# Attention and feed-forward kernel on one core: a shorter prologue, copies moved to ScalarE, and a new rule for filler matmuls

## Chip, cores and metric

One core of a Trainium2 (trn2) chip. The metric is device time in microseconds (us) of one execution, taken over several executions. A run counts as slow when it is over 1.5% above the fastest run of the same kernel; only fast runs are compared here unless a sentence says otherwise. A span (first to last instruction of the profiled execution) is about 2 us shorter than the device time of the same run (1036.2 against 1037.95 us before, 1008.3 against 1010.06 after).

Engine names as the profile prints them: PE is TensorE (matmuls), PEld its weight loads, ACT is ScalarE, DVE is VectorE, POOL is GpSimd, SP is the engine that issues most DMAs (27 of the 29 on the page of the kernel before).

## The reference, cut to what matters

```python
# x: [1, 2048, 512] bf16; 32 query heads of 16, one shared K/V head of 16; F = 1792
xn = layernorm(x)
q = (xn @ wq) -> 32 heads;  k = xn @ wk;  v = xn @ wv
p = softmax(q k^T * 16**-0.5)          # 32 x 2048 x 2048 exponentials
s = (p v) @ wo
g = silu(silu(xn @ w1) @ w2)
out = x + s * g
```

The softmax needs 32 x 2048 x 2048 exponentials, and ScalarE computes all of them.

## The kernel before

The sequence is cut into 4 chunks of 512 queries; four heads make a group, so there are 8 groups per chunk. A **unit** is a piece of the scores: 4 PSUM banks (even units) or 2 banks (odd units), 512 columns per bank. There are 683 units. Even units use banks 0 to 3, odd units banks 4 and 5; bank 6 gathers the output of a group, bank 7 serves **jobs**: all other matmul work (Q of later chunks `q`, both feed-forward layers `h` and `z`, output projection `w`), cut into parts of two matmuls that are strewn between units.

In each step PE computes the scores of unit idx+2, multiplies the finished exponentials of unit idx by V, and does a job part if one is due:

```python
for idx in range(min(2, NU)):
    emit_S(idx, NFILL_START)             # 3 fillers
for idx in range(MAXU):
    if idx < NU:
        if idx + 2 < NU:
            emit_S(idx + 2, nfill_for(idx))
        emit_PV(idx)
    for (n, pi) in parts_at_unit.get(idx, []):
        emit_job_part(n, pi)

def emit_S(u, nfill=0):
    if u >= 2:
        pe.wait_ge(act_sem.sem, u - 1)   # exp of unit u-2 has emptied these banks
    # ... 4 or 2 score matmuls; then, into the last bank:
    for fi in range(nfill):              # a zero weight: adds 0, costs PE time
        h = pe.matmul(bank(b0 + k), lhsT=zero_sb, rhs=xnT_sb[:, 0, 0:NQ], start=False, ...)
    h.then_inc(s_sem.sem, 1)             # the exp of unit u waits for this

def nfill_for(idx):
    nmm = sum(len(job_parts[n][pi]) for (n, pi) in parts_at_unit.get(idx, []))
    target = NFILL_START if idx < N_START else (NFILL if idx <= last_part_unit else NFILL_TAIL)
    return max(0, target - nmm)          # 3 at the start, 1 in the middle, 2 in the tail
```

A **filler** is a matmul with a zero weight. It keeps PE busy (0.39 us is recorded for one, 0.82 for three in a row, in the timelines below), and it stands between the scores and the semaphore that lets their exp begin. (The fillers of scores u are chosen from the job parts at step u-2.)

ScalarE's loop is one exp per unit, and a tanh (for the feed-forward part) behind some of them:

```python
a.wait_ge(s_sem.sem, u + 1)
a.activation(p_sb[...], ps[:, b0 * 512:(b0 + n) * 512], ACT.Exp).then_inc(act_sem.sem, 1)
for jn in cons_at_unit.get(u, []): emit_tanh(jn)
```

The prologue before these loops: layer norm, transposes of half 0 of the tokens, K of half 0, V, Q of group 0; then the same for half 1, with K and V in banks 0 to 2 again; then Q of groups 1 to 5 through banks 3 and 4. VectorE does every copy out of PSUM. Groups 6 and 7 of Q are jobs.

```python
NGP = 6 if NT > NT0 else NG
NGB = min(NGP, 3)
# ... PE:
for g in range(NGB, NGP):
    pe.wait_ge(qev_sem.sem, g)           # VectorE has copied the last Q out of bank 3
    emit_Q(g, 3)
qev_needed_for_bank = {2 + g: g + 1 for g in range(1, NGB)}
if NGP > NGB:
    qev_needed_for_bank[3] = NGP         # unit 0 needs bank 3
```

The softmax here doesn't subtract the row's maximum and nothing guards it: scores larger than these inputs give would overflow.

## Time and profile before

The first timing gave 1038.83 us (median of 5 runs, 1035.72 to 1043.29). The profiled execution has a span of 1036.2 us:

| stretch of the profiled execution | us |
|---|---|
| start to exp 0 | 47.51 |
| exp 0 to the start of the last exp | 974.01 |
| last exp to the end | 14.64 |

From the page of the kernel before. The first lines give busy time and its share of the span. The two rows of digits show the busy tenths of ACT and the granted PE clock in 40 slices of the span. The lower lines are groups of instructions: line, engine, operation, output and input, shape, count, then busy us and mean ns, then idle time of the engine just before them.

```profile
span 1036.2 us, 12801 instructions
...
PE 812.2 (78%) x5323; PEld 223.8 (22%) x5426; DVE 201.3 (19%) x356; ACT 972.6 (94%) x776; POOL 10.4 (1%) x13
...
ACT  4199999999999999999999999999999999999994
...
PEclk9999999999999999999989999999978999999999
...
L522 ACT ACTIVATE p_sb<-ps 128x1024 bf16<-128x1024 f32 (+1 forms) x683 | 949.8, 1573 | 36.4 <-PE ps L628 26.6
...
L628 PE MATMUL ps<-xnT_sb,zero_sb 128*128 128x512 bf16 x435 | 153.7, 392 | 2.7 <-issue 2.7
```

ACT is busy 94% of the time, and of its 36.4 us of idle time before exps 22.3 came before the first. The 78% of PE is not a sign of a full PE: 153.7 us of it are the fillers of L628.

**ScalarE's floor.** The records of single exps overlap: a four-bank exp's lasts 1998 ns on average, but the next exp can start 1757 ns after it. What counts is the distance from one start to the next, read from the trace's start times: 1757 ns after a four-bank exp, 904 ns after a two-bank exp, 477 ns after a tanh, when nothing is late. The trace has 341 four-bank and 342 two-bank exps, and the last, a two-bank one, has no distance after it: 341 x 1757 + 341 x 904 + 72 x 477 ns = 941.7 us. What a distance has above these values is called **excess** below. Summed over the stage the excess is 32.1 us: 0.9 in units 0 to 5, 17.3 in units 6 to 572, 13.8 in units 573 to 682, where no jobs are left.

The end of the prologue, timeline of the kernel before. Columns: start us, duration us, engine, line, operation, output and input, shape, count, and in brackets how long the engine was idle before and what released it.

```profile
34.33 2.56 PE L550 MATMUL ps<-xnT_sb,wkp_sb 128*128 128x512 bf16 x8 [2.58 <-DVE xnT_sb L361]
...
37.97 2.11 PE L566 MATMUL ps<-xnT_sb,wqp_sb 128*128 128x512 bf16 x7 [0.23 <-issue]
...
44.51 1.04 PE L566 MATMUL ps<-xnT_sb,wqp_sb 128*128 128x512 bf16 x4 [0.78 <-DVE qT_sb L375]
...
45.58 0.69 DVE L375 TENSOR_SCALAR qT_sb<-ps 128x512 bf16<-128x512 f32 x1 [1.13 <-PE ps L566]
...
46.33 0.39 PE L622 MATMUL ps<-qT_sb,kT_sb 32*128 32x512 bf16 x1 [0.46 <-DVE qT_sb L375]
...
47.51 2.79 ACT L522 ACTIVATE p_sb<-ps 128x2048 bf16<-128x2048 f32 x2 [22.28 <-PE ps L628]
```

K of half 1 begins at 34.33 us. Q group after Q group follows, each waiting for VectorE to copy out the one before (the bracket of the line at 44.51 names `DVE qT_sb`). Three of unit 0's four score matmuls start; the fourth, at 46.33, waits for the last Q to leave bank 3. The exp follows at 47.51.

One pair of units in the tail, timeline of the kernel before. The two lines of L622 with x4 are the starts of two consecutive four-bank scores:

```profile
1006.05 0.39 PE L622 MATMUL ps<-qT_sb,kT_sb 32*128 32x512 bf16 x4 [0.46 <-ACT p_sb L522]
...
1006.37 0.61 PE L628 MATMUL ps<-xnT_sb,zero_sb 128*128 128x512 bf16 x2
...
1008.95 0.40 PE L622 MATMUL ps<-qT_sb,kT_sb 32*128 32x512 bf16 x4 [0.46 <-ACT p_sb L522]
```

A pair takes 2.90 us here, against 1757 + 904 ns = 2.66 us of ScalarE work. In the start times of the exps the distance after a two-bank exp is 1128 ns in this stretch, 224 late. In units 495 to 504, which have no jobs either but one filler instead of two, it is 913.

Stretches of the kernel before. Columns: stretch and its length, busy us and instructions of PE, PEld, DVE, ACT and POOL, then the mean granted PE clock, the DMA share and GB/s:

```profile
746.00:766.00 20.00, 14.19 (x102) 4.18 (x102) 3.41 (x6) 20.00 (x17) 0.00 (x0) 1.00 0.00 0
766.00:786.00 20.00, 19.53 (x85) 3.83 (x86) 2.79 (x5) 17.64 (x13) 0.00 (x0) 0.50 0.00 1
884.00:1012.00 128.00, 105.56 (x691) 27.29 (x702) 11.17 (x20) 122.62 (x89) 0.00 (x0) 1.00 0.00 1
```

From 766 to 786 us the granted clock is a half. In those 20 us ACT is busy only 17.64. The clock records hold five such spells inside the exp stage, 37.5 us together; the longest, 20.5 us, is this one.

### The profile page before, as it was taken

The page shows a single profiled execution, that of the slowest core. Times are in us where ns is not written, and L with a number is a line of the kernel's source. Part 1 is how long each engine was busy: PE and PEld are TensorE (multiplying, and loading weights), DVE is VectorE, ACT ScalarE, POOL GpSimd, SP SyncE. Part 2 cuts the span into 40 slices and gives each one's busy share as a digit, 9 for nine tenths or more (in the row PEclk, how much of TensorE's full clock was granted, in tenths as well). Part 3 has the DMA queues.
Part 4 walks back from the last instruction along what each step waited for, and adds up shares of the span by engine and source line. Part 5 has one row for each costly group of instructions (what it writes and reads, how often), then busy time and mean ns, then how long its engine had stood idle before and what let it go on. Part 6 is the DMA issues. An engine that isn't in the chain of part 4 may idle for free.

```text
span 1036.2 us, 12801 instructions
## 1 busy us (share of the span) xinstructions
PE 812.2 (78%) x5323; PEld 223.8 (22%) x5426; DVE 201.3 (19%) x356; ACT 972.6 (94%) x776; POOL 10.4 (1%) x13
## 2 busy tenths in 40 slices
PE   1787778777788887778888877778889888888886
PEld 1322222222222222222222222222222222222222
DVE  7312222211211222121112212221101211100112
ACT  4199999999999999999999999999999999999994
POOL 4000000000000000000000000000000000000000
PEclk9999999999999999999989999999978999999999
DMA  9000000000000000000000000000000000000000
GB/s 265 1 1 1 1 1 1 1 1 1 1 1 6 16 2 1 1 1 1 1 1 16 6 1 1 1 1 2 1 1 11 11 1 1 1 1 1 2 1 20
DMA packets 7369, 9.76 MB, mean 9 GB/s; under 512 B 1488, under 2 KB 6608, under 8 KB 7312
## 3 DMA queue, kind: packets, MB, share of 16 engines
q1 hardware_dynamic: 6576, 5.28, 1.9%
q0 software_dynamic: 736, 3.67, 1.0%
q8 instruction: 42, 0.69, 0.3%
q14 instruction: 15, 0.12, 0.0%
HBM read 6.85 MB, written 2.10 MB: 9 GB/s over the span
## 4 chain that ended last, share of the span: by engine, by line
ACT 46%; PE 35%; issue 14%; DVE 4%; DMA 0%; ACTq 0%; another core or an unknown queue 0%; DVEq 0%
ACT p_sb L522 43%; PE ps L622 12%; PE ps L647 9%; PE ps L628 6%; ACT t_sb L512 3%; PE ps L686 2%; PE ps L679 2%; PE ps L711 1%; PE ps L692 1%; DVE stats_sb L337 1%; DVE oraw_sb L396 1%; PE ps L550 1%; PE ps L739 1%; PE ps L566 1%; DVE xnT_sb L361 0%
## 5 line engine op out<-in xcount | busy, mean ns | idle before, releaser
L522 ACT ACTIVATE p_sb<-ps 128x1024 bf16<-128x1024 f32 (+1 forms) x683 | 949.8, 1573 | 36.4 <-PE ps L628 26.6
L622 PE MATMUL ps<-qT_sb,kT_sb 32*128 32x512 bf16 x2048 | 272.3, 391 | 167.1 <-ACT p_sb L522 163.8
L647 PE MATMUL ps<-p_sb,vaug_sb 128*32 128x512 bf16 x2048 | 278.7, 396 | 16.4 <-DVE oraw_sb L396 7.9
L628 PE MATMUL ps<-xnT_sb,zero_sb 128*128 128x512 bf16 x435 | 153.7, 392 | 2.7 <-issue 2.7
L622 PEld LDWEIGHTS ps<-qT_sb,kT_sb 32*128 32x128 bf16 x2048 | 66.7, 91 | 412.5 <-ACT p_sb L522 383.7
L647 PEld LDWEIGHTS ps<-p_sb,vaug_sb 128*32 128x32 bf16 x2048 | 68.8, 93 | 193.0 <-issue 151.7
L431 DVE SCALAR_TENSOR_TENSOR u_sb<-t_sb,ps 128x512 bf16<-128x512 bf16 x56 | 38.3, 684 | 246.3 <-ACT t_sb L512 246.3
L396 DVE CAST oraw_sb<-ps 128x512 bf16<-128x512 f32 x32 | 22.1, 691 | 252.4 <-PE ps L647 252.4
L686 PE MATMUL ps<-w_sb,u_sb 128*128 128x512 bf16 x208 | 64.8, 387 | 3.8 <-issue 2.1
L679 PE MATMUL ps<-xnT_sb,w_sb 128*128 128x512 bf16 x203 | 64.1, 389 | 0.2 <-issue 0.2
L512 ACT ACTIVATE t_sb<-ps 128x512 bf16<-128x512 f32 x72 | 58.6, 815 | 0.0
L628 PEld LDWEIGHTS ps<-xnT_sb,zero_sb 128*128 128x128 bf16 x482 | 37.1, 96 | 85.5 <-issue 84.8
L442 DVE TENSOR_SCALAR qT_sb<-ps 128x512 bf16<-128x512 f32 x26 | 17.9, 688 | 107.7 <-PE ps L692 87.9
L435 DVE SCALAR_TENSOR_TENSOR tmp_sb<-t_sb,ps 128x512 bf16<-128x512 bf16 x16 | 10.9, 680 | 141.0 <-ACT t_sb L512 141.0
L692 PE MATMUL ps<-xnT_sb,wqp_sb 128*128 128x512 bf16 x93 | 29.9, 394 | 0.5 <-issue 0.5
L711 PE MATMUL ps<-wop_sb,xn_sb 128*128 128x512 bf16 x91 | 29.2, 400 | 0.8 <-issue 0.8
L415 DVE SCALAR_TENSOR_TENSOR fin_sb<-ps,tmp_sb 128x512 bf16<-128x512 f32 x16 | 11.0, 687 | 61.7 <-PE ps L711 58.3
L398 DVE STREAM_TRANSPOSE otr_sb<-oraw_sb 128x512 bf16<-128x512 bf16 x32 | 22.8, 712 | 1.1
L411 DVE STREAM_TRANSPOSE xn_sb<-otr_sb 128x512 bf16<-128x512 bf16 x32 | 22.8, 711 | 1.1
L686 PEld LDWEIGHTS ps<-w_sb,u_sb 128*128 128x128 bf16 x224 | 12.7, 97 | 27.8 <-issue 25.4
L679 PEld LDWEIGHTS ps<-xnT_sb,w_sb 128*128 128x128 bf16 x224 | 12.8, 97 | 25.7 <-issue 25.7
L539 PE MATMUL ps<-ident,xn_sb 128*128 128x128 bf16 x64 | 5.5, 266 | 12.7 <-DVE xn_sb L353 12.7
(46 smaller groups left out, 128.2 us busy)
## 6 DMA issues: line engine op xcount, KB each, us to landing
w_sb<-in_B_w_dram POOLq DMA_DIRECT2D x2, 1792.0 KB, 14.0
x_sb<-in_A_x_dram SPq DMA_DIRECT2D x4, 512.0 KB, 5.4
out_dram<-ob_sb SPq DMA_DIRECT2D x16, 128.0 KB, 1.7
wqn_sb<-in_A_wq_dram SPq DMA_DIRECT2D x1, 512.0 KB, 7.8
wop_sb<-in_A_wo_dram SPq DMA_DIRECT2D x4, 128.0 KB, 7.5
wkn_sb<-in_A_wk_dram SPq DMA_DIRECT2D x1, 16.0 KB, 6.8
wv_sb<-in_A_wv_dram SPq DMA_DIRECT2D x1, 16.0 KB, 6.5
```

The source lines that it names most:

```text
L396: v.tensor_copy(oraw_sb[:, sl, :], bank(OB)).then_inc(o_sem.sem, 1)
L398: v.transpose(otr_sb[:, sl, :], oraw_sb[:, sl, :]).then_inc(dv.sem, 1)
L431: v.scalar_tensor_tensor(out=u_sb[:, tc % 2, ft, :], in0=t_sb[:, ti % 2, :], scalar=1.0, in1=bank(FB), op0=ALU.add, op1=ALU.mult).then_inc ...
L512: a.activation(t_sb[:, ti % 2, :], bank(FB), ACT.Tanh, scale=scale).then_inc(t_sem.sem, 1)
L522: a.activation(p_sb[:, u % NPB, 0:n * NQ], ps[:, b0 * 512:(b0 + n) * 512], ACT.Exp).then_inc(act_sem.sem, 1)
L622: h = pe.matmul(bank(b0 + k), lhsT=kT_sb[32 * i:32 * i + KP, kt * P:(kt + 1) * P], rhs=qT_sb[32 * i:32 * i + KP, c % 2, g, :], start=True, ...
L628: h = pe.matmul(bank(b0 + k), lhsT=zero_sb[:, :], rhs=xnT_sb[:, 0, 0:NQ], start=False, stop=(fi == nfill - 1))
L647: h = pe.matmul(bank(OB)[32 * i:32 * (i + 1), :], lhsT=vaug_sb[:, kt, :], rhs=p_sb[:, u % NPB, k * NQ:(k + 1) * NQ], start=(kt == 0), stop ...
L679: h = pe.matmul(bank(FB), lhsT=w1_sb[:, dc, ft * P:(ft + 1) * P], rhs=xnT_sb[:, dc, tc * NQ:(tc + 1) * NQ], start=(dc == 0), stop=(dc == N ...
L686: h = pe.matmul(bank(FB), lhsT=u_sb[:, tc % 2, ft, (tt % 4) * P:(tt % 4 + 1) * P], rhs=w2_sb[:, ft, :], start=(ft == 0), stop=(ft == NFT - 1))
L692: h = pe.matmul(bank(FB), lhsT=wqp_sb[:, dc, g, :], rhs=xnT_sb[:, dc, c * NQ:(c + 1) * NQ], start=(dc == 0), stop=(dc == NDC - 1))
L711: h = pe.matmul(bank(FB), lhsT=on_sb[:, (c % 2) * NG + g, (tt % 4) * P:(tt % 4 + 1) * P], rhs=wop_sb[:, g, :], start=(g == 0), stop=(g == ...
```

## The change

Three things at once. (1) Only Q of groups 0 and 1 is computed ahead of the loop; groups 2 to 5 become jobs. (2) Half 1 uses banks of its own (4 to 7), and ScalarE, not VectorE, copies V, Q and the K of half 1 out of PSUM; waits for these copies are placed where a bank or value is first used. (3) A unit step without job parts gets 1 filler if even and 3 if odd.

```diff
-    NGP = 6 if NT > NT0 else NG
-    NGB = min(NGP, 3)
+    BIG = NT > NT0
+    NGP = 2 if BIG else NG
@@ VectorE: the copies of V, Q and half-1 K are removed @@
@@ ScalarE, after its normalisation work and the load of the Exp table @@
+            a_evac_V(0, 2)
+            a_evac_Q(0, 3)
+            if BIG:
+                for c in range(NC0, NC):
+                    a.wait_ge(kp_sem.sem, c + 1)
+                    a.activation(kT_sb[:, c * NQ:(c + 1) * NQ], bank(4 + c - NC0), ACT.Copy).then_inc(kev2_sem.sem, 1)
+                a_evac_V(1, 6)
+                a_evac_Q(1, 7)
@@ PE @@
                 for c in range(NC0, NC):
-                    emit_K(c, c - NC0)
-                emit_V(1, 2)
-                for g in range(1, NGB):
-                    emit_Q(g, 2 + g)
+                    emit_K(c, 4 + c - NC0)
+                emit_V(1, 6)
+                emit_Q(1, 7)
-            for g in range(NGB, NGP):
-                pe.wait_ge(qev_sem.sem, g)
-                emit_Q(g, 3)
@@ waits for banks 4 to 7 and for half 1 of K and V move to their first use (cut) @@
             def nfill_for(idx):
                 nmm = sum(len(job_parts[n][pi]) for (n, pi) in parts_at_unit.get(idx, []))
+                if nmm == 0:
+                    return 1 if idx % 2 == 0 else 3
                 target = ...
             for idx in range(min(2, NU)):
-                emit_S(idx, NFILL_START)
+                emit_S(idx, 1 if idx == 0 else NFILL_START)
```

More of the change, by code (lines that the diff above doesn't have):

```diff
@@ L266, in bass_recurrent_scan__grouped_kv_mqa__dense_activation_silu__prompt_kernel @@
         kev_sem = S_("kev")
+        kev2_sem = S_("kev2")
         vp_sem = S_("vp")
@@ L361, in evac_T @@
                     v.tensor_copy(xnT_sb[:, dc, ta * P:tb * P], src_).then_inc(xt_sem.sem, 1)
-            def evac_K(c, b):
-                v.wait_ge(kp_sem.sem, c + 1)
-                v.tensor_copy(kT_sb[:, c * NQ:(c + 1) * NQ], bank(b)).then_inc(kev_sem.sem, 1)
-            def evac_V(half, b):
-                ta, tb = halves[half]
-                v.wait_ge(vp_sem.sem, half + 1)
-                vps = bank(b).rearrange("p (t e) -> p t e", e=32)[:, 0:tb - ta, 0:DH]
-                v.tensor_copy(vaug_sb[:, ta:tb, 0:DH], vps).then_inc(vev_sem.sem, 1)
-            def evac_Q(g, b):
-                v.wait_ge(qp_sem.sem, g + 1)
-                v.tensor_scalar(qT_sb[:, 0, g, :], bank(b), QSCALE, None, op0=ALU.mult).then_inc(qev_sem.sem, 1)
             evac_T(0)
             for c in range(NC0):
-                evac_K(c, c)
-            evac_V(0, 2)
-            evac_Q(0, 3)
+                v.wait_ge(kp_sem.sem, c + 1)
+                v.tensor_copy(kT_sb[:, c * NQ:(c + 1) * NQ], bank(c)).then_inc(kev_sem.sem, 1)
             if len(halves) > 1:
                 evac_T(1)
-                for c in range(NC0, NC):
-                    evac_K(c, c - NC0)
-                evac_V(1, 2)
-            for g in range(1, NGB):
-                evac_Q(g, 2 + g)
-            for g in range(NGB, NGP):
-                evac_Q(g, 3)
             marks["xt_total"] = NDC * len(halves)
@@ L500, in _, with a_evac_V, a_evac_Q @@
             a.activation(scr_sb[:, 0:1], rstd_sb[:, 0:1], ACT.Exp)
+            def a_evac_V(half, b):
+                ta, tb = halves[half]
+                a.wait_ge(vp_sem.sem, half + 1)
+                vps = bank(b).rearrange("p (t e) -> p t e", e=32)[:, 0:tb - ta, 0:DH]
+                a.activation(vaug_sb[:, ta:tb, 0:DH], vps, ACT.Copy).then_inc(vev_sem.sem, 1)
+            def a_evac_Q(g, b):
+                a.wait_ge(qp_sem.sem, g + 1)
+                a.activation(qT_sb[:, 0, g, :], bank(b), ACT.Copy, scale=QSCALE).then_inc(qev_sem.sem, 1)
+            a_evac_V(0, 2)
[6 more added lines that the diff above has]
+                a_evac_Q(1, 7)
+            else:
+                for g in range(1, NGP):
+                    a_evac_Q(g, 3)
             def emit_tanh(n):
@@ L574, in _ @@
             emit_Q(0, 3)
-            if len(halves) > 1:
+            if BIG:
                 emit_transposes(1)
                 pe.wait_ge(xt_sem.sem, 2 * NDC)
-                pe.wait_ge(kev_sem.sem, NC0)
-                pe.wait_ge(vev_sem.sem, 1)
-                pe.wait_ge(qev_sem.sem, 1)
                 for c in range(NC0, NC):
-                    emit_K(c, c - NC0)
-                emit_V(1, 2)
-                for g in range(1, NGB):
-                    emit_Q(g, 2 + g)
-            else:
-                pe.wait_ge(qev_sem.sem, 1)
-                for g in range(1, NGB):
-                    emit_Q(g, 2 + g)
-            for g in range(NGB, NGP):
-                pe.wait_ge(qev_sem.sem, g)
-                emit_Q(g, 3)
-            pe.wait_ge(qev_sem.sem, 1)
-            pe.wait_ge(vev_sem.sem, len(halves))
-            pe.wait_ge(kev_sem.sem, NC)
-            pe.wait_ge(xt_sem.sem, marks["xt_total"])
-            qev_needed_for_bank = {2 + g: g + 1 for g in range(1, NGB)}
-            if NGP > NGB:
-                qev_needed_for_bank[3] = NGP
+                    emit_K(c, 4 + c - NC0)
+                emit_V(1, 6)
+                emit_Q(1, 7)
+            else:
+                for g in range(1, NGP):
+                    pe.wait_ge(qev_sem.sem, g)
+                    emit_Q(g, 3)
+            pe.wait_ge(qev_sem.sem, NGP if not BIG else 1)
+            pe.wait_ge(vev_sem.sem, 1)
+            pe.wait_ge(kev_sem.sem, NC0)
+            pe.wait_ge(xt_sem.sem, marks["xt_total"])
+            bank_free_need = {}
+            if BIG:
+                for c in range(NC0, NC):
+                    bank_free_need[4 + c - NC0] = (kev2_sem, c - NC0 + 1, ("kbank", c))
+                bank_free_need[6] = (vev_sem, 2, ("vbank",))
+                bank_free_need[7] = (qev_sem, 2, ("qbank",))
             waited = set()
@@ L618, in emit_S @@
                         need(qev_sem, g + 1, ("qev", g))
-                    if (b0 + k) in qev_needed_for_bank:
-                        need(qev_sem, qev_needed_for_bank[b0 + k], ("qbank", b0 + k))
+                    kc = kt // 4
+                    if BIG and kc >= NC0:
+                        need(kev2_sem, kc - NC0 + 1, ("kev2", kc))
+                    if (b0 + k) in bank_free_need:
+                        sm, cnt, key = bank_free_need[b0 + k]
+                        need(sm, cnt, key)
                     last = (k == nk - 1)
@@ L635, in emit_PV @@
                 pe.wait_ge(act_sem.sem, u + 1)
-                if OB in qev_needed_for_bank:
-                    need(qev_sem, qev_needed_for_bank[OB], ("qbank", OB))
+                if OB in bank_free_need:
+                    sm, cnt, key = bank_free_need[OB]
+                    need(sm, cnt, key)
                 h = None
@@ L640, in emit_PV @@
                     gi = grp_index[(c, g)]
+                    if BIG and kt >= NT0:
+                        need(vev_sem, 2, ("vev2",))
                     if kt == 0 and gi > 0:
@@ L663, in emit_job_part @@
                 if pi == 0:
-                    if FB in qev_needed_for_bank:
-                        need(qev_sem, qev_needed_for_bank[FB], ("qbank", FB))
+                    if FB in bank_free_need:
+                        sm, cnt, key = bank_free_need[FB]
+                        need(sm, cnt, key)
                     if n >= 1:
```

## The prediction

> **What bounds the kernel now.** ScalarE. In the busy table ACT has 94% (972.6 of 1036.2 us). The table of instruction groups gives 683 exps and 72 tanhs. ACT idles only 36.4 us before exps, 22.3 of it before the first: the timeline shows exp 0 at 47.51 us, the last at 1021.5, and a 14 us tail. Start-to-start times of ACT instructions, from the trace: 1757 ns after a four-bank exp, 904 after a two-bank exp, 477 after a tanh when nothing is late. 342 x 1757 + 341 x 904 + 72 x 477 gives 943.5 us; the exp stage takes about 975. So about 32 us inside the stage and part of the 47.5 us ahead of it can be won; the rest is ACT's floor.
>
> **Term 1, the prologue: -7.4 us.** Before: second-half K matmuls start at 34.3 us, V ends at 37.7, then five Q groups follow, the last three in a ping-pong between PE and VectorE (1.82 us each); exp 0 waits for the last (bank 3 is reused). After: only Q0 and Q1 are done ahead. Q1's matmuls should end near 39.2 us, ACT's copy (0.8 us, as the 128x512 tanh reads PSUM) near 40.0; exp 0 starts near 40.1. The copies of V, Q and second-half K move onto ACT where it idled (25.2 to 47.5 us). Q2 to Q5 become four loop jobs: VectorE is 19% busy and PE has room; no ACT time. I expect no added table load: [...] the trace agrees so far (copies after the first load add none).
>
> **Term 2, fewer fillers ahead of four-bank scores: -12.8 us.** Fillers sit between the scores and their semaphore. Four-bank scores must finish inside a two-bank exp (904 ns). With two fillers (units 573 to 682, after the last job) the interval is 1128 ns, 225 lost; with one (units 493 to 504) 913, 9 lost. After: one there, three on odd units, which have 1757 ns. 55 x 216 ns = 11.9 us. Units 0 to 5 (three fillers, 440 lost twice) give 0.9.
>
> **Term 3, fewer cold spells: -5 us, uncertain (0 to -9).** The granted clock drops to half five times inside the exp stage, 37.5 us in all; 20.5 us of that at 766 to 786 us, where there are no jobs and one filler per unit. There four-bank scores lose 576 ns each. About 10 us of excess lies in such spells. [...] Job-free units get two fillers on average instead of one, so most spells should go. The extra two fit: scores 0.32, three fillers 0.65, PV 0.32 make 1.3 us (estimate from the timeline) against 1.757.
>
> **Sum.** 1038.8 - 7.4 - 12.8 - 5 = 1013.6 us. Range 1008 to 1020. Faster by over 2%: 0.80; within 2%: 0.19; slower: 0.01.
>
> **What would show it.** Exp 0 near 40 us; the last near 996; in the last 110 units a pair takes 2.67 us, not 2.90; halved-clock time in the stage under 15 us; ACT idle before exps, after the first, from 14 us to under 5; tail unchanged.
>
> **What would make it wrong.** Cold spells stay or lengthen: three fillers at half clock (about 2.3 us of work) would outlast a four-bank exp. Exp 0 later because ACT's copies queue. If term 3 gives nothing, the gain is 1.9%, inside "same".

## The result, and the profile after

After: 1010.92 us median (1009.99 to 1012.59, 8 runs). Before, in all 15 runs up to then: 1037.17 us median (1035.17 to 1043.29). The ratio of the fast runs is 0.9742, 95% interval 0.9724 to 0.9760: faster by 2.6%. Ratios in this document are those on record, from means of fast runs, so they are not quite the ratio of the medians quoted beside them (means of the listed runs give the same to within 0.0007).

The page of the kernel after, the same lines:

```profile
span 1008.3 us, 13241 instructions
...
PE 843.6 (84%) x5542; PEld 239.0 (24%) x5647; DVE 198.3 (20%) x350; ACT 968.6 (96%) x782; POOL 10.4 (1%) x13
...
ACT  4599999999999999999999999999999999999994
...
PEclk8999999999999999999999999999999999999999
...
L522 ACT ACTIVATE p_sb<-ps 128x1024 bf16<-128x1024 f32 (+1 forms) x683 | 944.5, 1589 | 2.0 <-PE ps L629 0.9
...
L629 PE MATMUL ps<-xnT_sb,zero_sb 128*128 128x512 bf16 x655 | 197.6, 384 | 1.7 <-issue 1.7
```

The span fell by 27.9 us. ACT's idle time before exps fell from 36.4 to 2.0 us. The largest piece left the list because ACT now does copies in the prologue, so its wait there is no longer counted before the exp; inside the stage it went from 14.1 to 2.0. The PEclk row has no dip inside the exp stage. There are 655 recorded fillers instead of 435, and 44 us more filler time on PE, and yet the kernel is faster.

The end of the prologue, timeline of the kernel after:

```profile
34.30 1.90 PE L550 MATMUL ps<-xnT_sb,wkp_sb 128*128 128x512 bf16 x8 [2.58 <-DVE xnT_sb L362]
...
37.06 0.81 PE L566 MATMUL ps<-xnT_sb,wqp_sb 128*128 128x512 bf16 x3
...
37.90 0.60 ACT L488 ACTIVATE qT_sb<-ps 128x512 bf16<-128x512 f32 x1 [0.60 <-PE ps L566]
...
38.55 2.79 ACT L522 ACTIVATE p_sb<-ps 128x2048 bf16<-128x2048 f32 x2
```

Exp 0 starts at 38.55 us instead of 47.51; Q1 is the last thing that ScalarE copies before it, in 0.60 us.

One pair in the tail, timeline of the kernel after; the fillers (L629) are one behind the four-bank scores and three behind the two-bank scores:

```profile
900.66 0.40 PE L623 MATMUL ps<-qT_sb,kT_sb 32*128 32x512 bf16 x4 [0.24 <-ACT p_sb L522]
...
900.99 0.39 PE L629 MATMUL ps<-xnT_sb,zero_sb 128*128 128x512 bf16 x1
...
901.96 0.82 PE L629 MATMUL ps<-xnT_sb,zero_sb 128*128 128x512 bf16 x3
...
903.34 0.40 PE L623 MATMUL ps<-qT_sb,kT_sb 32*128 32x512 bf16 x4 [0.24 <-ACT p_sb L522]
```

Four-bank scores start 2.68 us apart instead of 2.90, close to ScalarE's 2.66. The rest is 16 ns after each four-bank exp (1773 ns in both kernels' tails) and 9 after each two-bank exp (913).

Stretches of the kernel after:

```profile
766.00:786.00 20.00, 17.58 (x121) 4.79 (x122) 2.98 (x6) 20.00 (x16) 0.00 (x0) 1.00 0.04 14
846.00:984.00 138.00, 121.75 (x800) 35.65 (x814) 14.64 (x26) 137.30 (x104) 0.00 (x0) 1.00 0.00 1
```

The same stretch of time, 766 to 786 us, has the full clock, and ACT is busy throughout. In the tail (last line) PE is busy 121.75 of 138 us (88%), before it was 105.56 of 128 (82%).

The fall of the span, term by term, all from the start times of exps in the two traces:

| part | before | after | change, us | predicted |
|---|---|---|---|---|
| start to exp 0 | 47.51 | 38.55 | -8.96 | -7.4 |
| excess, units 0 to 5 | 0.94 | 0.08 | -0.86 | -0.9 |
| excess, units 573 to 682 | 13.84 | 2.48 | -11.36 | -11.9 |
| excess, units 6 to 572 | 17.34 | 10.68 | -6.66 | -5 |
| excess after tanhs | 0.15 | 0.08 | -0.07 | none |
| last exp to the end | 14.64 | 14.65 | +0.01 | 0 |

### The profile page after: what moved, and what is told of

The parts are those of the page before. It is cut to its first block, busy times and chain, and to the rows that moved or that the text cites. A ratio compares the mean times of both kernels' runs of the same rounds, so it can differ in the third digit from the quotient of the medians.

```text
span 1008.3 us, 13241 instructions
## 1 busy us (share of the span) xinstructions
PE 843.6 (84%) x5542; PEld 239.0 (24%) x5647; DVE 198.3 (20%) x350; ACT 968.6 (96%) x782; POOL 10.4 (1%) x13
## 4 chain that ended last, share of the span: by engine, by line
ACT 44%; PE 33%; issue 18%; DVE 4%; DMA 0%; ACTq 0%; DVEq 0%
ACT p_sb L522 39%; PE ps L623 11%; PE ps L651 9%; PE ps L629 8%; ACT t_sb L512 5%; PE ps L697 2%; PE ps L691 1%; DVE stats_sb L338 1%; DVE oraw_sb L375 1%; PE ps L716 1%; PE ps L746 1%; PE ps L550 1%; DVE xnT_sb L362 0%; DMA x_sb<-in_A_x_dram 0%; DVE mv_sb L341 0%
## 5 line engine op out<-in xcount | busy, mean ns | idle before, releaser
L623 PE MATMUL ps<-qT_sb,kT_sb 32*128 32x512 bf16 x2048 | 267.3, 385 | 106.5 <-ACT p_sb L522 103.0
L651 PE MATMUL ps<-p_sb,vaug_sb 128*32 128x512 bf16 x2048 | 274.4, 390 | 17.4 <-DVE oraw_sb L375 8.4
L629 PE MATMUL ps<-xnT_sb,zero_sb 128*128 128x512 bf16 x655 | 197.6, 384 | 1.7 <-issue 1.7
L629 PEld LDWEIGHTS ps<-xnT_sb,zero_sb 128*128 128x128 bf16 x703 | 53.9, 97 | 100.7 <-issue 80.0
L421 DVE TENSOR_SCALAR qT_sb<-ps 128x512 bf16<-128x512 f32 x30 | 20.5, 684 | 108.2 <-PE ps L697 108.2
L697 PE MATMUL ps<-xnT_sb,wqp_sb 128*128 128x512 bf16 x109 | 33.8, 384 | 1.8 <-issue 1.8
## 6 DMA issues: line engine op xcount, KB each, us to landing
w_sb<-in_B_w_dram POOLq DMA_DIRECT2D x2, 1792.0 KB, 14.1
```

What stands on the lines that cost most here:

```text
L623: h = pe.matmul(bank(b0 + k), lhsT=kT_sb[32 * i:32 * i + KP, kt * P:(kt + 1) * P], rhs=qT_sb[32 * i:32 * i + KP, c % 2, g, :], start=True, ...
L629: h = pe.matmul(bank(b0 + k), lhsT=zero_sb[:, :], rhs=xnT_sb[:, 0, 0:NQ], start=False, stop=(fi == nfill - 1))
L651: h = pe.matmul(bank(OB)[32 * i:32 * (i + 1), :], lhsT=vaug_sb[:, kt, :], rhs=p_sb[:, u % NPB, k * NQ:(k + 1) * NQ], start=(kt == 0), stop ...
L697: h = pe.matmul(bank(FB), lhsT=wqp_sb[:, dc, g, :], rhs=xnT_sb[:, dc, c * NQ:(c + 1) * NQ], start=(dc == 0), stop=(dc == NDC - 1))
```

## The experiments

All kernels gave the correct result. They ran on several chips; each ratio is against the kernel before on the same chip. The theory: the gain is the sum of three independent things, an earlier exp 0, fewer fillers ahead of four-bank scores, and fewer half-clock spells because PE is busier. Rivals: the prologue is nearly the whole gain; what matters in the prologue is ScalarE making the copies; fillers only delay; or only their number matters.

| run | edit | median us (range) | ratio to before (95%) |
|---|---|---|---|
| e1 | new prologue, old fillers | 1025.78 (1024.55 to 1033.50) | 0.9886 (0.9846 to 0.9926) |
| e2 | old prologue, new fillers | 1018.73 (1018.07 to 1022.92) | 0.9814 (0.9775 to 0.9853) |
| e3 | before, two Q groups ahead | 1025.49 (1024.89 to 1026.11) | 0.9874 (0.9840 to 0.9907) |
| e6 | before, three odd fillers | 1032.15 (1031.93 to 1033.48) | 0.9941 (0.9907 to 0.9975) |
| e4 | after, one filler everywhere | 1044.80 (1038.53 to 1101.09; two slow runs) | 1.0042 (1.0000 to 1.0084) |
| e5 | after, two fillers everywhere | 1032.14 (1031.63 to 1032.94) | 0.9942 (0.9908 to 0.9975) |
| e7 | before, odd fillers in one stretch | 1033.64 (1031.35 to 1038.39) | 0.9960 (0.9924 to 0.9995) |
| e8 | after, both ends reordered | 1006.55 (1006.17 to 1007.31) | 0.9696 (0.9666 to 0.9725) |
| e9 | after, one odd filler in the tail | 1042.31 (1041.15 to 1043.64) | 1.0049 (0.9998 to 1.0100) |
| e10 | e4 once more, for its profile | 1049.20 (one run) | none |
| e11 | after, once more | 1011.42 (1011.08 to 1012.16) | 0.9726 (0.9705 to 0.9747) |
| e12 | e2 once more, beside e11 | 1020.13 (1018.98 to 1022.81) | 0.9812 (0.9788 to 0.9836) |

### e1: the new prologue with the old fillers

```diff
 # against after
-                if nmm == 0:
-                    return 1 if idx % 2 == 0 else 3
-                emit_S(idx, 1 if idx == 0 else NFILL_START)
+                emit_S(idx, NFILL_START)
```

> The new prologue (two Q groups ahead, copies on ScalarE, other banks) with the old filler rule. Theory (three separate terms): exp 0 starts at 38.5 to 40 us, and the time falls by 7.5 to 9 us, ratio about 0.992; the last 110 units keep the 1128 ns interval after two-bank exps, and halved-clock spells stay inside the exp stage. Rival (the prologue is nearly the whole gain): a fall of 20 us or more, ratio 0.981 or less.

Measured: 1025.78 us, ratio 0.9886. Exp 0 at 39.92 us, as the theory said; the tail keeps its 1128 ns. The rival is refuted: this is well short of the gain of the whole change. But the fall is larger than the 7.6 us of the earlier exp 0: in the traces the stage itself shrank too, from 974.0 to 968.5 us, and the half-clock time inside it fell from 37.5 to 6.8 us although no filler was added. The fast runs of e1 had granted clocks of 0.977 to 0.996, those of before in the same rounds 0.964 to 0.994. The reason that the traces suggest is that Q2 to Q5 are now jobs: the jobs that follow come 12 to 16 units later, and so the job-free stretch that was steps 489 to 513 is only 501 to 513. The three terms are not independent.

### e2: the old prologue with the new fillers

```diff
 # against before
+                if nmm == 0:
+                    return 1 if idx % 2 == 0 else 3
-                emit_S(idx, NFILL_START)
+                emit_S(idx, 1 if idx == 0 else NFILL_START)
```

> The old prologue with the new filler rule. Theory: exp 0 stays near 46.5 to 47.5 us, the stage from exp 0 to the last exp shrinks from 974 to about 955 us, no halved-clock spells in it; a fall of 18 to 19 us, ratio about 0.982. Rival (the prologue is nearly the whole gain): a fall under 5 us, ratio above 0.995.

Measured: 1018.73 us, ratio 0.9814, exp 0 at 47.01 us, the stage 956.9 us. One spell of 3.4 us is left, at 49 us, where exps have just begun. The filler rule alone is the larger part of the gain: every run of e2 is faster than every run of e1 on the same chip.

### e3: two Q groups ahead, and nothing else

```diff
 # against before
-    NGP = 6 if NT > NT0 else NG
+    NGP = 2 if NT > NT0 else NG
```

> The kernel before with one number changed: two Q groups ahead instead of six; the copies stay on VectorE and the banks are reused as before. Theory (what shortens the prologue is the deferral of four Q groups): exp 0 at 39.5 to 41.5 us, a fall of 6 to 8 us, ratio about 0.993, within 1.5 us of the full new prologue. Rival (moving the copies to ScalarE and to separate banks is what counts): exp 0 not before 44 us, a fall under 3 us.

Measured: 1025.49 us, the same as e1 on the same chip. The fall (ratio 0.9874, 13 us) is larger than the 6 to 8 us expected, as in e1: the half clock inside the stage is 10.2 us in e3's trace. The end of the prologue, timeline of e3:

```profile
37.59 0.81 PE L566 MATMUL ps<-xnT_sb,wqp_sb 128*128 128x512 bf16 x3
...
38.44 0.69 DVE L375 TENSOR_SCALAR qT_sb<-ps 128x512 bf16<-128x512 f32 x1 [0.59 <-PE ps L566]
...
39.18 0.39 PE L622 MATMUL ps<-qT_sb,kT_sb 32*128 32x512 bf16 x1 [0.46 <-DVE qT_sb L375]
...
40.36 1.88 ACT L522 ACTIVATE p_sb<-ps 128x2048 bf16<-128x2048 f32 x1 [15.06 <-PE ps L628]
```

VectorE still copies, bank 3 is still reused, and the fourth score matmul still waits for it (39.18). From the start of Q1's matmuls to exp 0 it takes 2.77 us (37.59 to 40.36), in e1's trace 1.92 (38.00 to 39.92). So the deferral of four Q groups is what shortens the prologue; the move of the copies to ScalarE and the separate banks are worth about 0.9 us of it in the traces, which the times do not resolve. The rival is refuted.

### e6: three fillers in odd units, even units as they were

```diff
 # against before
+                if nmm == 0 and idx % 2 == 1:
+                    return 3
```

> The kernel before with three fillers in job-free odd units alone; even units keep one (two in the last 110). Theory (idle PE time brings the halved-clock spells, and they cost time): halved-clock time inside the exp stage falls from 37.5 us to under 8, the time falls by 3 to 9 us, ratio 0.991 to 0.997, while the last 110 units keep the 1128 ns interval. Rival (fillers only delay; the spells cost nothing or come at random): no change or slower, ratio 0.998 or more.

Measured: 1032.15 us, ratio 0.9941, and no half-clock time in the stage of its profile. The tail keeps its 224 ns per pair. More fillers, put where ScalarE has slack, made the kernel faster by themselves. Compared unit by unit with the profile of before, the middle lost 6.5 us of excess: in three units near the ends of groups (323, 492, 556) the excess grew by 1.5 us in sum, and in the others it fell by 8.0, nearly all of it in the spells. That small growth was not pursued.

The kernel before points the same way without any edit. Its 38 runs beside these experiments, all fast, range from 1032.66 us (granted clock 0.994) to 1044.10 us (0.967); clock and time correlate with -0.88, and a line through them has a slope of 3.6 us per 0.01 of clock. Much of its spread between runs goes with lost clock. The kernel after, with granted clocks of 0.991 to 0.998 in the runs of e11, spreads over 1.1 us.

### e4 and e10: one filler in every job-free unit

```diff
 # against after
-                    return 1 if idx % 2 == 0 else 3
+                    return 1
```

> The kernel after with one filler in every job-free unit, odd ones too (the delay ahead of four-bank scores stays as in after, the number of fillers in those units halves). Theory (odd fillers pay by keeping the clock up): halved-clock spells return, above all in the last 110 units, which have no jobs; each such pair loses about 576 ns; the time is 10 to 35 us above after, 1021 to 1046 us. Rival (fillers only delay, fewer is never worse): as fast as after or 1 to 2 us faster, 1008 to 1011 us, few or no spells.

> The one-and-one kernel once more, unchanged, for a profile that is not of the slow state. Theory: a time of 1038 to 1046 us as its fast runs had, 80 to 110 us of halved clock inside the exp stage (granted clock 0.90 to 0.93), most of it in the last 150 us. Rival: the halved clock lies elsewhere, for example in the first 100 us.

Measured: e4's fast runs 1038.53 to 1044.95 us, 28 to 34 us above the median of the kernel after; two of six runs were slow (1054.72 and 1101.09), and its profile fell into the slowest, so it is not used. e10, a single run and so of unknown state, gave a profile of 1049.20 us with clock 0.895: 203.0 us of half clock inside the stage, more than the 80 to 110 expected, 172 of them at the end (from 858.5 us on). The time is 3 us above the range that was expected. The rival (fillers only delay, so fewer are never worse) is refuted: of all these kernels this one has the fewest fillers (355 by the rule, against 482 before and 703 after) and the longest time.

### e9: one odd filler in the last 110 units only

```diff
 # against after
-                    return 1 if idx % 2 == 0 else 3
+                    return 1 if idx % 2 == 0 or idx > last_part_unit else 3
```

> The kernel after with one filler instead of three in odd units of the last 110 units alone; all before unit 573 as in after. Theory (the odd fillers keep the clock up where there are no jobs): halved-clock spells come back in the last 150 us and nowhere else; 576 ns per four-bank score in a spell, so 5 to 30 us above after, 1016 to 1041 us. Rival (one filler each is enough, the slow runs of the one-and-one kernel had another cause): within 2 us of after, no spells.

Measured: 1042.31 us, 31 us above the kernel after and a little above what was expected. Stretches of e9:

```profile
38.50:864.00 825.50, 704.52 (x4588) 191.96 (x4674) 157.90 (x261) 823.50 (x659) 0.00 (x0) 1.00 0.01 3
864.00:1023.00 159.00, 152.18 (x663) 30.58 (x675) 11.17 (x20) 135.34 (x98) 0.00 (x0) 0.50 0.00 1
```

From exp 0 to 864 us the stage is as in after (10.6 us of excess in units 6 to 572 against 10.7), and the clock is full. Then it halves and stays at a half to the end of the stage. A pair of units there, timeline of e9:

```profile
900.17 0.61 PE L623 MATMUL ps<-qT_sb,kT_sb 32*128 32x512 bf16 x4
...
900.72 0.61 PE L629 MATMUL ps<-xnT_sb,zero_sb 128*128 128x512 bf16 x1
...
901.36 2.79 ACT L522 ACTIVATE p_sb<-ps 128x2048 bf16<-128x2048 f32 x2 [0.46 <-PE ps L629]
...
903.42 0.61 PE L623 MATMUL ps<-qT_sb,kT_sb 32*128 32x512 bf16 x4
```

A pair takes 3.25 us, 0.57 more than after. At half clock scores (0.54 us), filler (0.53) and the steps of the semaphores no longer fit into a two-bank exp (904 ns), and ScalarE idles 0.46 us per pair. Note that PE is busy 152.18 of 159 us in this stretch, 96%, and the clock does not come back.

### e5: two fillers in every job-free unit

```diff
 # against after
-                    return 1 if idx % 2 == 0 else 3
+                    return 2
```

> The kernel after with two fillers in every job-free unit: as many fillers as after, so as much PE work, but one more ahead of the four-bank scores. Theory (placement counts): no halved-clock spells, yet the interval after two-bank exps in the last 110 units is 1128 ns again, 11 to 12 us in all, and some 10 us more in job-free units of the middle; the time is 12 to 30 us above after. Rival (only the number of fillers counts, through the clock): within 2 us of after.

Measured: 1032.14 us, 21 us above the kernel after, with no half-clock time in the stage. The pair in the tail, timeline of e5:

```profile
901.15 0.39 PE L623 MATMUL ps<-qT_sb,kT_sb 32*128 32x512 bf16 x4 [0.46 <-ACT p_sb L522]
...
901.47 0.61 PE L629 MATMUL ps<-xnT_sb,zero_sb 128*128 128x512 bf16 x2
...
904.05 0.40 PE L623 MATMUL ps<-qT_sb,kT_sb 32*128 32x512 bf16 x4 [0.46 <-ACT p_sb L522]
```

Four-bank scores start 2.90 us apart, as in the kernel before, and are late again: 12.4 us of excess after two-bank exps in the tail as in the kernel before, and 16.4 against 6.1 us in the middle. The same number of fillers, other places: the rival that only the number counts is refuted.

### e7: odd fillers only in the longest job-free stretch

```diff
 # against before
+                if nmm == 0 and idx % 2 == 1 and 489 <= idx <= 512:
+                    return 3
```

> The kernel before with three fillers in the odd job-free units 491 to 514 alone, the stretch where its trace shows the longest halved-clock spell. Theory (the 20.5 us spell there comes of the missing jobs): no halved-clock spell in that stretch, 3 to 5 us less than before, and less spread between runs than before has. Rival (the spell's place is chance): another long spell elsewhere or the same one, no change beyond 1 us.

Measured: ratio 0.9960 (0.9924 to 0.9995), about 4 us less. The spell of 20.5 us is gone from the profile, and PE is busy 17.96 of 20 us from 746 to 766 instead of 14.19. A spell of 10.2 us at 532 us is left. The spread is 7.0 us against 10.5 us of before in the same rounds, which is a weak sign with six runs. This fits the theory that the missing jobs made that spell, but does not prove it. For it speaks that e10's trace has a spell of 20.5 us at the same place of the stage (from 756.1 us, 717 us after exp 0; before, 718). But e1's trace, with one filler per unit in its job-free stretch as in e10, has no spell there: such a stretch makes a spell possible, not certain.

### e11 and e12: the prologue where the clock is already up

Both kernels are unchanged (after, and e2's), side by side on one chip.

> The kernel after, unchanged, on one chip with the fillers-only kernel. Theory (the new prologue is worth its earlier exp 0 where the fillers already keep the clock up, and more than that only where spells are left to remove): 7.0 to 9.0 us below the fillers-only kernel of this call. Rival (the extra 4 us that the prologue alone showed against before belongs to the prologue itself): 11 to 13 us below it.

> The fillers-only kernel (old prologue, new filler rule), unchanged, beside the kernel after on the same chip. Theory: 1018 to 1020 us, exp 0 at 46.5 to 47.6 us, 7.0 to 9.0 us above the kernel after. Rival: 11 to 13 us above it.

Measured: 1011.42 and 1020.13 us, 8.7 us apart in the medians. Exp 0 starts at 39.68 and 47.05 us, 7.4 apart. With the spells removed by the fillers, the prologue is worth roughly its earlier exp 0. In the two traces the stages differ by 1.8 us more (956.8 and 955.1 us); e12's has a spell of 3.4 us soon after exp 0. This is what the theory expected; e1's larger fall included spells that the fillers would have removed anyway.

e11's trace also explains the 8.96 us of the first profile. In e11 the clock is at a half from 34.4 to 37.8 us, as it was in the profile of before (35.4 to 38.8 us); in the first profile of after it was not, and exp 0 came 1.1 us earlier. Such a spell at the end of the prologue is not bound to a kernel: of the traces with the old prologue before, e2, e6 and e12 have it and e7 does not; of the two traces of after, one has it.

### e8: what is left at the two ends

```diff
 # against after. PE, prologue: unit 0 first, while VectorE copies xnT of half 1
                 emit_transposes(1)
+                pe.wait_ge(kev_sem.sem, NC0); pe.wait_ge(vev_sem.sem, 1); pe.wait_ge(qev_sem.sem, 1)
+                emit_S(0, 1)
                 pe.wait_ge(xt_sem.sem, 2 * NDC)
 # ScalarE: the exp of unit 0 right after a_evac_Q(0, 3), ahead of the half-1 K copies
 # PE, tail: output tiles 0 and 1 are finished before tiles 2 and 3 are begun
+            wo_part(0, range(NG - 1)); wo_part(1, range(NG - 1))
+            pe.wait_ge(on_sem.sem, NG * NC)
+            for k in (0, 1): wo_part(k, [NG - 1]).then_inc(wo_sem.sem, 1)
+            for k in (2, 3): wo_part(k, range(NG)).then_inc(wo_sem.sem, 1)
```

> The kernel after with unit 0's scores and exp moved ahead of the second-half K matmuls (ScalarE idles there), and in the tail the last product of output tiles 0 and 1 ahead of tiles 2 and 3. Theory (ScalarE's floor plus a prologue and a tail is the whole time): exp 1 starts where exp 0 did, 1.6 to 1.8 us saved; the tail shrinks from 14.65 to about 11.9 us; together 4 to 4.7 us below after, 1006 to 1007 us on an equal chip. Rival (something else, such as jobs, holds the stage): under 2 us saved.

In the kernel before (and after) the tail multiplies seven groups of all four output tiles first. The tail, timeline of the kernel before:

```profile
1022.92 6.22 PE L739 MATMUL ps<-wop_sb,xn_sb 128*128 128x512 bf16 x27
...
1025.25 0.71 DVE L411 STREAM_TRANSPOSE xn_sb<-otr_sb 128x512 bf16<-128x512 bf16 x1
...
1029.39 0.69 DVE L415 SCALAR_TENSOR_TENSOR fin_sb<-ps,tmp_sb 128x512 bf16<-128x512 f32 x1 [3.43 <-PE ps L745]
```

The last group was ready at 1025.96 us, but VectorE's final step could start only at 1029.39, behind 28 matmuls. The two ends of e8:

```profile
32.82 1.88 ACT L494 ACTIVATE p_sb<-ps 128x2048 bf16<-128x2048 f32 x1 [1.84 <-PE ps L610]
...
39.39 2.79 ACT L524 ACTIVATE p_sb<-ps 128x1024 bf16<-128x1024 f32 x2 [0.48 <-PE ps L610]
```

```profile
993.76 0.39 PE L657 MATMUL ps<-p_sb,vaug_sb 128*32 128x512 bf16 x2 [0.52 <-ACT p_sb L524]
...
996.41 0.71 DVE L390 STREAM_TRANSPOSE xn_sb<-otr_sb 128x512 bf16<-128x512 bf16 x1
...
997.61 0.69 DVE L394 SCALAR_TENSOR_TENSOR fin_sb<-ps,tmp_sb 128x512 bf16<-128x512 f32 x1 [0.48 <-PE ps L754]
```

Measured: 1006.55 us, ratio 0.9696, 4.4 us below the median of the kernel after. Exp 0 now runs in ScalarE's idle time at 32.82, and exp 1 starts at 39.39, about where exp 0 starts in the traces of after (38.55 and 39.68). VectorE's final step begins 0.49 us after the last group's transpose, and the tail is 11.99 us instead of 14.65. This version beats both kernels.

## Why the prediction was right

The prediction was 1013.6 us (1008 to 1020), from a first timing of before of 1038.83; the measured medians were 1010.92 and 1037.17. All three mechanisms showed in the traces and runs. That the sum came within 3 us is in part luck: term 3 was sized from one profile of a kernel whose spells differ from run to run, and a spell in the prologue moves exp 0 by 1.1 us.

**Term 1, the prologue, predicted 7.4 us, 9.0 in the first pair of profiles, 7.4 to 8.7 by e11 and e12.** The mechanism was right, and e3 shows that the deferral carries it. Two sizes were off. ScalarE's copy took 0.60 us, not the 0.8 taken from the tanh, whose record (815 ns on average) overlaps the exp before it, by 0.39 us in the median of the 72 in the trace of before. And Q1's matmuls ended about 1.3 us earlier than in the estimate, which had carried over the half clock of before's prologue; with that spell in the trace (e11) exp 0 starts at 39.68 against the predicted 40.1. No table load was added: there are two in the trace of after, 1283 ns each, as before, and none after the one at 23.67 us, although ScalarE makes its copies (29.10 to 38.50 us) between that load and exp 0.

**Term 2, fillers ahead of four-bank scores, predicted 12.8, measured 12.2.** 1128 became 913 ns in the tail, to the nanosecond what one filler showed in units 495 to 504. e5 shows that their place did it: with as many fillers, but two there, the tail loses the same 12.4 us again.

**Term 3, spells, predicted 5, measured 6.7 net in the middle of the stage.** Half-clock time in the stage went from 37.5 us to none. e6 shows the term alone, 0.9941 or about 6 us. That more fillers would remove most spells was the author's estimate, and the prediction counted the term as an effect of the fillers only; the traces of e1 and e3 (6.8 and 10.2 us of half clock in the stage, without added fillers) suggest that the four new jobs also remove spells. So the terms must not be measured one by one and added: e1 and e2 together would give 0.9886 x 0.9814 = 0.9702, against 0.9742 measured, a difference that points the right way but lies within their intervals. The traces and e11 and e12 carry that point, not this product.

**What the prediction had underrated** is how much hangs on the odd fillers. It named three fillers at half clock as the danger (its 2.3 us is the author's estimate). e9 and e10 show the other side as the larger risk: with one filler in the odd units too, the tail alone costs about 30 us (in e9's trace 28.1 of excess in units 573 to 682 and 1.9 after the last exp, against after) and the kernel is no faster than before. (Lowering only the even fillers, to one even and two odd in the tail, was not run.)

**What stays open.** Four of the five spells of before lie outside the long job-free stretch, and why the clock halved at those units and not at others with the same pattern is settled only in part. The kept traces show more when the stages (all but e4's) are cut into windows of 3.413 us in step with the clock records. (That is the shortest spell in them; in the trace of before the full-clock stretches from the first spell of the stage to the last are 43, 34, 22 and 8 times as long.) In each of the 14 windows just before a spell, fillers and job parts together streamed for at most 0.43 us, the time of two; that holds for only 80 of the 3535 full-clock windows that no spell followed. In each of the 14 windows at the end of which the full clock came back, they streamed for at least 1.18 us, nearly three at half clock; that holds for only 2 of the 112 after which the half clock stayed. So a window with at most two such matmuls preceded each of these spells but did not always bring one, and e9's two per 3.25 us seldom reach three in a window. This is a count made after the fact, and no run tested it. It is an estimate: weight loads stand for the matmuls, at 0.21 us each as fillers in a row follow each other in the timelines (one lasts 0.39 us, three 0.82), and 0.43 at half clock.

Also open: 10.7 us of excess is left in units 6 to 572 of the kernel after; some of it sits at units near group ends (596 ns at unit 492, 580 at 556), and none of it was taken apart by an experiment. e8 was not taken apart either: its two halves are told apart by the trace only.

## What to carry to other kernels

When one engine is the floor, write down its start-to-start times when nothing is late, and sum what each instruction has above them; here that gave the second term to within 0.6 us before anything was built (12.8 predicted, 12.2 measured). Filler work has a place as well as an amount: put it behind the step with the most slack (odd units, 1757 ns) and take it from ahead of the step with the least (904 ns). When a change takes work away from a PE that is idle in parts, check the granted clock in the same look, since a lost clock can cost more than the delay that was saved: here 28 us of excess in the tail (e9) against the 11.4 won there.

## What the traces show of the clock and of the table load

- PE was idle only in short pieces before the longest spell: in the kernel before, from 746 to 766 us, PE's idle brackets in the timeline of the last job-free pairs are 0.68 us each, PE is busy 14.19 of 20 us (71%), and then the clock halves for 20.5 us. Stretches with PE busy 75% (210 to 250 us of before), 82% (tail of before) and 88% (tail of after) kept the full clock. The busy share may not be the right measure: what told the windows before a spell from most others here was the count of fillers and job matmuls in them, at most two (see "What stays open").
- A busy PE did not bring the full clock back: in e9 PE was busy 152.18 of 159 us (96% by the profile's modelled ends) and the clock stayed at a half for 163.8 us. Spells last 3.4, 6.8, 20.5 (all before) and 163.8 us (e9), all multiples of 3413 ns, the shortest.
- A table load took 1283 ns. In the trace of after the load for Exp starts at 23.67 us, 0.01 us after the last activation, and the next activation starts at 24.96, 0.01 us after its end.
